# Recurrent attention and two feed-forward layers on one core: S of both batch halves in one step, a last group of sixteen, and a new order

## The chip, the core and the metric

The kernel runs on one core of a Trainium2 chip. Its engines are TensorE (PE in the profile; its weight loads are PEld), VectorE (DVE), ScalarE (ACT), GpSimd (POOL) and the DMA queues, which SyncE (SP) issues for the most part. The metric is the time of one execution on the device in microseconds; a number of runs is given by its median.

## The reference

```python
for t in range(S):                      # B, H, S, D = 2, 8, 768, 40
    m_new = np.maximum(f_gate[:, :, t] + m, i_gate[:, :, t])
    f_stab, i_stab = np.exp(f_gate[:, :, t] + m - m_new), np.exp(i_gate[:, :, t] - m_new)
    C = f_stab * C + i_stab * outer(v[t], k[t]);  n = f_stab * n + i_stab * k[t];  m = m_new
    y[:, :, t] = sigmoid(o_gate) * (C @ q[t]) / max(abs(n @ q[t]), 1)
x = y as (1536, 320)
x = ((x @ w1) * (x @ w2)) @ w3 @ w_out      # w1, w2: 320 x 1024; w3: 1024 x 1024; w_out: 1024 x 320
h = x @ w_in                                # 320 x 2048
out = (h * tanh(softplus(h))) @ w_out2      # 2048 x 320
```

All in float32. In lines 3 to 5 the indices are shortened.

## The kernel before

The sequence is cut into six chunks of 128 steps; a chunk of one of the two batch halves is a unit, so there are twelve (unit 2c + b is chunk c of half b). Per unit TensorE makes E (exponents of the decay, lines 618 to 625), S (products of k and q, lines 645 to 651: eight products on 40 rows, two heads at a time in the two halves of the array), I (state times q), U (the state's update, 40 columns, two at a time), Y (weights times v) and X (transposes). ScalarE takes the exponential of E into w (dw), VectorE multiplies S into w (wg, lines 653 to 656) and adds up the state, GpSimd makes vw, the gating by o and, from unit 8 on, the mask. Two units make 256 columns of a block of 512 tokens; there are three blocks.

The first layer then runs with float32 split into a rounded high and a low part: A and B (psa, psb, lines 1066 to 1076) are x with w1 and w2, W (psw) is w3 with w_out, X1 (psx) brings them together. The second layer (from line 1159) has 48 matrices of 128 by 512, sixteen in each block: H (psh, lines 1163 to 1187) makes two at once in the two halves of the array, ScalarE applies mish twice (line 1191 in the rounded format, line 1195 in full), VectorE takes the difference (gl), and O (pso, lines 1201 to 1213) multiplies both with w_out2 into four banks. They go in groups of eight: H of four pairs, then eight O (lines 1228 to 1241). Each weight piece is loaded and cleaned up on ScalarE and VectorE; its rounded half is made on ScalarE (hi), its low half on VectorE or GpSimd by a table (ENG).

The order on every engine is set by a planner when the program is built (Work.plan, lines 247 to 345). Each step is a node with an engine, a duration, what it depends on and which slots it takes; among the nodes that could start within a slack of each other, the one with the smallest due time goes first. Due times stand in the table DUE or come from formulas. The planner knows of three forms of products on TensorE (whole array, half rows for S and H, few columns for U) and adds SWITCH where the form changes. Where it sees TensorE waiting, up to the last X, it puts filler products into bank b0 (keep_warm, lines 589 to 594, psz in the profile), whose result nobody reads:

```python
stop = t + (s - t) * TUNE["ff"]
while t + 2 * fill[1] < stop:
    t, k = self.products(t, fill[1], 0.94), k + 1
while k < 12 and guard and self.lacks(t, max(s, t), max(s, t) + last, self.share[n]):
    t1, t, k = t, self.products(t, fill[1], 0.94), k + 1
```

The second loop adds fillers where the planner's own account of TensorE's load would go under the value gd; it is zero here.

Of the kernel before, what the change touches and what calls it, by code (L numbers as in the profile page):

```python
# [19 lines left out]
NQK = 2  # L20
# [6 lines left out]
    sgg=(2, 4), mu=8, s_pe=0.268, s_act=0.368, s_dve=0.435, s_pool=0.232, ahead=1, w0n=5, ff=0.972, gd=0.0,  # L27
    ph=0.071, a0=-12.81, ap=-93.853, a_ld=-1652.39, e_e=8363.2, e_s=3345.95, e_r=2252.59, g_ld=6316.58,
    g1=-2898.98, g2=-4276.68, o_1=-7529.36, o_2=8885.52, c_ld=3037.46, c_wo=1113.52, cp_wo=108.045, p0=-952.74,
    pp0=59.804, c_12=-11722.61, w0=1316.87, wp=-59.276, c_w3=-13157.38, p1=-662.73, pp1=33.908, p2=704.76,  # L30
    pp2=572.165, x0=-2337.92, x_p=2487.93, x1=-2214.51, x2=2869.52, xp=-139.242, ldn={'w12': 2, 'wi': 2},
    c_o2=88.35, cp_o2=12.531, c_wi=-5894.32, c_o3=-2264.6, m0=232.0, grp=8, mp0=-162.897, mp=204.465, m_o=1263.83,
# [4 lines left out]
    lo_w3='POOL', lo_wi='POOL', lo_o2='DVE', lo_o3='DVE', xo='POOL', vw='POOL', dup='ACT', rb0='DVE', rc0='DVE',  # L37
    rb1='DVE', rc1='DVE', rb='ACT', rc='ACT', st0='DVE', cb0='DVE', prep='ACT', g_tt='DVE', g_ll='DVE',
    lo_w120='DVE', lo_w121='DVE', lo_w122='DVE', lo_w123='DVE', lo_w124='DVE', lo_w125='POOL', lo_w126='DVE',
# [5 lines left out]
    set_0=0.0, ld_o_0=0.6, ld_g=1.3, ld_qk_0=1.7, ld_kv_0=1.8, load_0=1.9, ld_o_1=4.6, lr_0=4.8, less_0=4.8,  # L45
    ll_0=4.5, la1_0=5.1, la0_0=5.4, rb_0=5.4, one_0=5.7, lb0_0=38.2, lb1_0=6.2, pl_1=6.3, rc_0=6.4, pl_0=6.9,
    E_0=6.8, pa_1=7.7, pr_1=6.8, pa_2=7.8, E_1=8.1, dw_0=8.4, ld_qk_1=8.7, pt_1=9.0, S_0=9.0, pt_2=9.4,
    ld_kv_1=21.3, pb_1=10.6, dw_1=10.7, pb_2=10.8, pc_1=11.4, pc_2=11.7, te_1=11.9, lr_1=11.9, turn_1=12.3,
    less_1=13.1, te_2=13.2, lr_2=14.2, less_2=13.5, load_1=13.3, turn_2=13.9, ll_2=13.9, la1_2=14.1, ll_1=14.5,
    sgm_0=14.7, ld_o_2=14.7, vw_0=14.7, lb1_2=13.6, U_0=-9.8, ld_qk_2=16.0, rb_1=11.7, wg_0=16.7, la0_2=16.0,  # L50
    sgm_1=17.3, vw_1=17.4, ld_kv_2=17.1, la1_1=15.2, st_0=17.9, Y_0=18.0, la0_1=14.2, mag_0=17.3, lb0_2=18.4,
    lb0_1=19.0, set_1=19.1, lb1_1=-2.1, rc_1=19.4, S_1=19.9, clamp_0=20.0, rb_2=20.5, cb_0=20.6, load_2=20.6,
    E_2=20.9, wg_1=21.1, xs_0=31.7, r1_0=20.8, mag_1=21.3, E_3=22.0, ld_o_3=22.2, r2_0=17.9, bits1_0=11.3,
    dw_2=21.8, U_1=22.9, r3_0=24.9, bits2_0=25.1, Y_1=23.3, ld_qk_3=23.3, st_1=26.1, xo_0=23.9, bits_0=26.7,
    ld_kv_3=24.4, dw_3=24.0, S_2=25.2, cb_1=24.6, vw_2=25.5, r1_1=25.3, I_2=23.7, rc_2=25.6, wg_2=26.5, U_2=27.8,
    xs_1=27.4, dx_2=26.8, dup_0=25.2, Ie_2=30.6, hi_0=27.0, E_4=28.5, load_3=30.2, st_2=36.5, Y_2=29.4, dw_4=30.0,
    r2_1=27.8, lo_0=29.0, r3_1=29.8, mag_2=29.3, clamp_1=29.4, xo_1=30.5, X_0=31.2, ld_qk_4=30.7, cb_2=29.2,
    E_5=24.6, Xe_0=30.1, clamp_2=29.0, dup_1=32.7, r1_2=30.9, Xl_0=25.0, xs_2=31.7, S_3=32.4, dw_5=29.5,
    ld_kv_4=32.0, r2_2=28.1, bits1_2=32.5, ld_o_4=33.0, I_3=33.4, r3_2=33.0, vw_3=33.1, bits2_2=33.7, X_1=34.5,
    dx_3=33.4, U_3=34.9, rb_3=34.0, wg_3=34.6, xo_2=35.8, Xe_1=35.1, Ie_3=36.2, Y_3=36.7, st_3=36.2, rc_3=35.9,  # L60
    ld_qk_5=36.6, Xl_1=37.1, dup_2=37.0, bits_2=37.7, S_4=31.0, ld_kv_5=38.0, cb_3=38.5, vw_4=35.9, hi_2=38.4,
    load_4=57.2, E_6=40.7, bits1_1=39.4, r1_3=39.2, r2_3=39.9, wg_4=40.2, xs_3=38.4, I_4=39.9, dw_6=35.6,
    ld_o_5=40.7, I_5=41.6, r3_3=55.0, ld_qk_6=41.2, dx_4=40.1, Ie_4=40.2, xo_3=41.4, Y_4=42.5, ld_kv_6=42.1,
    Ie_5=41.2, rb_4=41.9, lo_2=43.3, dx_5=58.4, dup_3=39.6, S_5=41.4, rc_4=43.9, cb_4=44.4, E_7=46.0, r1_4=44.2,
    bits2_1=45.2, mag_3=45.1, X_3=47.0, X_2=47.5, r2_4=44.8, dw_7=45.9, vw_5=43.9, r3_4=46.6, U_4=47.9,
    clamp_3=47.0, Xe_3=46.9, U_5=41.3, wg_5=46.9, Xe_2=47.3, sgm_2=47.7, ld_qk_7=31.9, st_5=47.7, Y_5=50.2,
    vw_6=49.4, ld_kv_7=49.4, st_4=50.2, Xl_3=52.0, S_6=51.9, cb_5=51.1, Xl_2=51.4, E_8=21.4, r1_5=45.7, xs_4=52.1,
    sgm_3=51.8, sgm_4=51.8, sgm_5=51.8, wg_6=39.5, A_0=53.4, dw_8=53.9, xs_5=50.9, ld_kv_8=25.0, r2_5=47.1,
    bits1_3=53.5, r3_5=49.7, vw_7=53.2, B_0=55.3, bits2_3=61.7, Ae_0=54.7, bits_1=55.6, I_7=57.1, ld_kv_9=56.1,
# [284 lines left out]
def dve(n):  # L354
    return 0.07 + n / 960
# [18 lines left out]
def kernel(  # L374
# [78 lines left out]
    def bank(name):  # L453
        return slot(psum, name, [128, 512])
# [892 lines left out]
```

## Time and profile before

| | us |
|---|---|
| three runs | 430.96, 420.09, 430.78 |
| their median | 430.78 |
| the profiled execution | 418.26 |
| its span | 416.5 |
| busy in the span: TensorE, VectorE, ScalarE, GpSimd | 409.1, 290.9, 198.1, 76.5 |

The span goes from the first to the last instruction of the profiled execution. The attention fills about its first 108 us, the first layer goes to 242, the second to the end. Matmuls overlap in the pipeline, so the time from start to start says what one costs; the duration in a row is longer.

### The profile page before, as it was taken

Reading aid. Unit: us, or ns where it says so; the run is one execution under the profiler, and the core shown is the slowest. Engines: PE = TensorE matmul, PEld = TensorE weight load, DVE = VectorE, ACT = ScalarE, POOL = GpSimd, SP = SyncE. Lnnn points to the kernel's source line nnn. Section 1 sums busy time; section 2 is a strip of 40 time slices with the busy share of each in tenths; the row PEclk is TensorE's granted clock in tenths of the full one; section 3 lists DMA queues with packets and bytes.
Section 4 is the critical chain, followed back from the end, with each engine's and each line's share of the span. In section 5 each row is a group of like instructions: output and inputs, shape, how many; then the busy total and the mean of one; then the engine's idle time right before and its main releaser. Section 6 shows DMA issues by size and latency. Waiting matters only on the chain.

```text
span 416.5 us, 7139 instructions
## 1 busy us (share of the span) xinstructions
PE 409.1 (98%) x2814; PEld 359.7 (86%) x2814; DVE 290.9 (70%) x527; ACT 198.1 (48%) x381; POOL 76.5 (18%) x78
## 2 busy tenths in 40 slices
PE   8899999999999999999999999999999999999996
PEld 5688888898888899988888888989989999889995
DVE  7989989998899959887999988889231041330221
ACT  8786976544534444452743366157051161340430
POOL 3144343345002232422001132300000000000000
PEclk9999999999999999999999999999999999999999
DMA  8965844542224533435324253420100000100002
GB/s 240 326 192 161 239 164 135 159 151 65 64 89 143 169 108 101 151 115 155 98 71 119 65 126 80 174 64 2 65 0 2 0 2 2 63 2 0 2 2 64
DMA packets 30497, 40.88 MB, mean 98 GB/s; under 512 B 1856, under 2 KB 24640, under 8 KB 30464
## 3 DMA queue, kind: packets, MB, share of 16 engines
q1 hardware_dynamic: 29952, 39.95, 31.5%
q10 hardware_dynamic: 512, 0.48, 0.3%
q8 instruction: 22, 0.36, 0.3%
q14 instruction: 11, 0.09, 0.1%
HBM read 38.45 MB, written 1.97 MB: 97 GB/s over the span
## 4 chain that ended last, share of the span: by engine, by line
PE 93%; DVE 4%; ACT 1%; DMA 1%; issue 0%; DVEq 0%
PE pso L1210 21%; PE psh L1186 20%; PE psa L1057 11%; PE psb L1057 11%; PE psw L1028 7%; PE psY L699 5%; PE psS L650 3%; PE psx L1097 3%; PE psx L1099 3%; PE psx L1098 3%; PE psI L661 2%; PE psx L1102 1%; PE psx L1101 1%; PE psE L624 1%; PE psX L743 1%; PE psE L623 1%
## 5 line engine op out<-in xcount | busy, mean ns | idle before, releaser
L410 DVE TENSOR_TENSOR gl<-u,gh 128x512 fp32r<-128x512 f32 x48 | 32.8, 691 | 68.6 <-ACT u L1195 68.5
L1191 ACT ACTIVATE gh<-psh 128x512 fp32r<-128x512 f32 x48 | 28.9, 601 | 79.4 <-PE psh L1186 79.4
L1186 PE MATMUL psh<-xd,wih 64*128 64x512 f32 x240 | 59.7, 394 | 0.0
L1186 PEld LDWEIGHTS psh<-xd,wih 64*128 64x128 f32 x240 | 43.8, 185 | 3.4
L502 DVE SCALAR_TENSOR_TENSOR f<-raw,f 128x640 int32<-128x640 int32 (+2 forms) x44 | 42.4, 964 | 0.7
L1210 PE MATMUL pso<-wo,gh 128*128 128x320 f32 x192 | 42.6, 310 | 0.0
L1186 PE MATMUL psh<-hs,wih 64*128 64x512 f32 x144 | 41.7, 395 | 0.0
L507 DVE SCALAR_TENSOR_TENSOR f<-raw,f 128x640 int32<-128x640 int32 (+2 forms) x44 | 36.1, 823 | 0.9
L410 POOL TENSOR_TENSOR th<-f,th 128x512 fp32r<-128x512 f32 x16 | 21.4, 1345 | 64.9 <-ACT th L512 59.9
L1210 PEld LDWEIGHTS pso<-wo,gh 128*128 128x128 f32 x192 | 32.0, 188 | 1.1 <-issue 1.1
L1186 PE MATMUL psh<-xd,wil 64*128 64x512 f32 x120 | 31.8, 391 | 0.0
L1186 PE MATMUL psh<-hs,wil 64*128 64x512 f32 x120 | 31.6, 391 | 0.0
L1210 PE MATMUL pso<-wo2h,gh 128*128 128x320 f32 x96 | 30.0, 312 | 0.0
L1210 PE MATMUL pso<-wo2h,gl 128*128 128x320 f32 x96 | 29.6, 309 | 0.0
L1210 PE MATMUL pso<-wo2l,gh 128*128 128x320 f32 x96 | 29.6, 309 | 0.0
L1210 PE MATMUL pso<-wo,gl 128*128 128x320 f32 x96 | 29.6, 309 | 0.0
L1195 ACT ACTIVATE u<-psh 128x512 f32<-128x512 f32 x48 | 29.0, 604 | 0.0
L1186 PEld LDWEIGHTS psh<-hs,wih 64*128 64x128 f32 x144 | 26.1, 184 | 3.2 <-issue 1.3
L1057 PE MATMUL psa<-hs,w12h 128*128 128x512 f32 x72 | 28.5, 395 | 0.0
L1057 PE MATMUL psb<-hs,w12h 128*128 128x512 f32 x72 | 28.4, 394 | 0.0
L1028 PE MATMUL psw<-woh,th 128*128 128x320 f32 x128 | 28.3, 309 | 0.0
L493 DVE TENSOR_SCALAR f<-f 128x640 f32<-128x640 f32 (+2 forms) x44 | 22.7, 517 | 6.6 <-ACT f L487 5.8
(146 smaller groups left out, 1028.5 us busy)
## 6 DMA issues: line engine op xcount, KB each, us to landing
raw<-in_w_dram SPq DMA_DIRECT2D x16, 512.0 KB
raw<-in_w_out_dram SPq DMA_DIRECT2D x12, 640.0 KB
raw<-in_w_dram SPq DMA_DIRECT2D x16, 384.0 KB
raw<-in_w_in_dram SPq DMA_DIRECT2D x16, 320.0 KB
kv<-in_kv_dram SPq DMA_DIRECT2D x12, 324.0 KB
qk<-in_qk_dram SPq DMA_DIRECT2D x24, 160.0 KB
sg<-in_o_gate_dram SPq DMA_DIRECT2D x12, 160.0 KB
out_dram<-yo SPq DMA_DIRECT2D x9, 160.0 KB
```

The source lines that it names most:

```text
L410: return eng.tensor_tensor(out=o, in0=a, in1=b, op=op)
L493: nc.vector.tensor_scalar(out=ff, in0=ff, scalar1=HI_MIN, scalar2=HI_MAX, op0=ALU.max, op1=ALU.min)
L502: nc.vector.scalar_tensor_tensor(out=f, in0=t["raw"][:, :, 1], scalar=-0x40000000, in1=f, op0=ALU.bitwise_and, op1=ALU.bitwise_or)
L507: nc.vector.scalar_tensor_tensor(out=f, in0=t["raw"][:, :, 0], scalar=29, in1=f, op0=ALU.logical_shift_right, op1=ALU.bitwise_or)
L650: nc.tensor.matmul(t["S"][g][:, p * T:(p + 1) * T], lhsT=t["qk"][rows, 1, p, :], rhs=t["qk"][rows, 0, p, :], start=True, stop=True)
L699: nc.tensor.matmul(ps[:, h * VW:(h + 1) * VW], lhsT=t["w"][:, h, :], rhs=t["v"][:, h, :], start=True, stop=True)
L1028: nc.tensor.matmul(ps, lhsT=t[a][:, 0, c * 128:(c + 1) * 128], rhs=wo[b], start=(c0 + c + s == 0), stop=(c0 + c == KC - 1 and s == 2))
L1057: nc.tensor.matmul(ps, lhsT=a, rhs=b, start=(n == 0 and not begun), stop=(n == len(seq) - 1))
L1186: nc.tensor.matmul(mt[i + k]["ps"], lhsT=w[k][:, c], rhs=x[k][c], start=(n == 0 and c == 0), stop=(n == 2 and c == KC2 - 1))
L1191: nc.scalar.activation(out=t["gh"], in_=t["ps"], func=AF.Mish)
L1195: nc.scalar.activation(out=t["u"], in_=t["ps"], func=AF.Mish)
L1210: nc.tensor.matmul(ps, lhsT=t[a][:, sl], rhs=wo[b], start=(ft == 0 and n == 0), stop=(ft == KF2 - 1 and n == 2))
```

## The change

- S of both halves of a chunk is one step from chunk 2 on (ss=2): it waits for the loads and the E of both units and takes four banks.
- The groups of the second layer are 0-8, 8-16, 16-24, 24-32 and 32-48 instead of six of eight; the last one's matrices get the slots of the dead first-layer result as well.
- The planner counts 0.2 us for a change of form instead of 0.1, prefers to stay in a form (fb), fills all of a wait that it sees (ff) and guards its account of the load (gd=0.299).
- The low halves of the last four w_out2 pieces are made on GpSimd, those of two w1/w2 pieces change places.
- The table DUE has new values, above all for the attention.

```diff
 TUNE = dict(
-    sgg=(2, 4), mu=8, s_pe=0.268, s_act=0.368, s_dve=0.435, s_pool=0.232, ahead=1, w0n=5, ff=0.972, gd=0.0,
+    sgg=(2, 4), mu=8, s_pe=0.301, s_act=0.359, s_dve=0.435, s_pool=0.0, ahead=1, w0n=5, ff=1.0, gd=0.299, ph=0.071,
...
-    c_o2=88.35, cp_o2=12.531, c_wi=-5894.32, c_o3=-2264.6, m0=232.0, grp=8, mp0=-162.897, mp=204.465, m_o=1263.83,
+    x0=-2337.92, x_p=2487.93, x1=-2214.51, x2=2869.52, xp=-139.242, ldn={'w12': 2, 'wi': 2}, c_o2=88.35,
+    cp_o2=12.531, c_wi=-5894.32, c_o3=-2264.6, m0=232.0, grp=(0, 8, 16, 24, 32, 48), mp0=-162.897, mp=204.465,
+    m_o=1263.83, ss=2, sw=0.2, fb=3.0,
...
 ENG = dict(
-    lo_w3='POOL', lo_wi='POOL', lo_o2='DVE', lo_o3='DVE', xo='POOL', vw='POOL', dup='ACT', rb0='DVE', rc0='DVE',
+    lo_w3='POOL', lo_wi='POOL', lo_o2='DVE', lo_o3='POOL', xo='POOL', vw='POOL', dup='ACT', rb0='DVE', rc0='DVE',
...
 DUE = dict(
-    ld_kv_1=21.3, pb_1=10.6, dw_1=10.7, pb_2=10.8, pc_1=11.4, pc_2=11.7, te_1=11.9, lr_1=11.9, turn_1=12.3,
+    ld_kv_1=21.3, pb_1=10.6, dw_1=9.5, pb_2=10.8, pc_1=11.4, pc_2=11.7, te_1=11.9, lr_1=24.6, turn_1=12.3,
...
-                    c = min((c for c in cand if c[0] <= s0 + TUNE.get(SLACK.get(e), 0.0)), key=lambda c: c[1])
+                    stay = TUNE["fb"] if e == "PE" else 0.0
+                    c = min((c for c in cand if c[0] <= s0 + TUNE.get(SLACK.get(e), 0.0)),
+                            key=lambda c: c[1] - (stay if self.form[c[2]] == form else 0.0))
...
             if e == "PE" and self.form[n] != form:
-                last += self.SWITCH
+                last += TUNE["sw"]
...
         tag = work.take()
+        if tag[0] == "y":
+            k, n = divmod(int(tag[1:]), 5)
+            h, l = xset["b", k]
+            return (h[:, n] if n < 3 else l[:, n - 3]).bitcast(F32)
...
         def S_():
-            t["S"] = [bank("psS") for _ in range(2)]
...
+            for t in (tl[x] for x in mine):
+                t["S"] = [bank("psS") for _ in range(2)]
...
-        node("S", "PE", -K["e_s"], 0.9, S_, [("ld_qk", u), ("E", u), ("Y", u - K["ahead"])], [at("wg"), at("wg")],
-             warm=0.45, form=1)
+        mine = [x for x in range(u - u % B, u - u % B + B)] if c >= K["ss"] else [u]
+        if u == mine[0]:
+            node("S", "PE", -K["e_s"], 0.9 * len(mine), S_,
+                 [(x, n) for n in mine for x in ("ld_qk", "E")] + [("Y", u - K["ahead"])],
+                 [(AT, [("wg", n)]) for n in mine for _ in range(2)], warm=0.45, form=1)
...
-        node("wg", "DVE", -3, 2 * dve(512), wg, [("S", u), ("dw", u), ("vw", u), ("ms", u)])
+        node("wg", "DVE", -3, 2 * dve(512), wg, [("S", mine[0]), ("dw", u), ("vw", u), ("ms", u)])
...
+    def group(i):
+        return next((a, b) for a, b in zip(K["grp"], K["grp"][1:]) if a <= i < b)
...
-        p, g = i // 2, i // K["grp"]
+        p = i // 2
+        g0, g1 = group(i)
+        last = kb == NBLK - 1
+        GP = places("z", 16) + (places("z", 6, 25) + places("y", 10)) * last
+        YP = places("z", 16) if last else places("z", 6, 25)
...
-                     [("H", p - 1), ("X2l", kb), ("B", NBLK * KF1 - 1), ("lo", wi_n[ft // 2]), ("O", g * K["grp"] - 1)],
+                     [("H", p - 1), ("X2l", kb), ("B", NBLK * KF1 - 1), ("lo", wi_n[ft // 2]), ("O", g0 - 1)],
```

In the order of TensorE this is what the prediction speaks of. First, S of units 4 and 5 (rows of both qk buffers), with Y of unit 3 ahead. Before:

```order
L675 MATMUL psU<-vw,kv 40x41 x8
L594 MATMUL psz<-causal,identr 128x512 x5
L699 MATMUL psY<-kv,w 128x41 x8
L650 MATMUL psS<-qk_78 128x128 x8
L661 MATMUL psI<-st_80,qk_78 128x82 x4
L664 MATMUL psI<-ex_r_90,ones_92 128x8
...
L699 MATMUL psY<-kv,w 128x41 x8
L675 MATMUL psU<-vw,kv 40x41 x8
L650 MATMUL psS<-qk_79 128x128 x8
```

After:

```order
L682 MATMUL psU<-vw,kv 40x41 x8
L668 MATMUL psI<-st_80,qk_78 128x82 x4
L671 MATMUL psI<-ex_r_90,ones_92 128x8
L600 MATMUL psz<-causal,identr 128x512 x2
L706 MATMUL psY<-kv,w 128x41 x8
L657 MATMUL psS<-qk_78 128x128 x8
L657 MATMUL psS<-qk_79 128x128 x8
...
L750 MATMUL psX<-ident,x 128x128 x3
L706 MATMUL psY<-kv,w 128x41 x8
```

Both S stand together behind Y of unit 3, where I, E, I, Y and U stood between them; the fillers ahead of Y of unit 3 are two and not five, and stand behind an I. Second, the stretch from U of units 5 and 4 on, after the change (before, it holds no filler):

```order
L682 MATMUL psU<-vw,kv 40x41 x16
L600 MATMUL psz<-causal,identr 128x512 x4
L682 MATMUL psU<-vw,kv 40x41 x8
L706 MATMUL psY<-kv,w 128x41 x8
...
L657 MATMUL psS<-qk_78 128x128 x8
L657 MATMUL psS<-qk_79 128x128 x8
L600 MATMUL psz<-causal,identr 128x512 x5
L630 MATMUL psE<-ex_r_90,ex_l_88 128x512 x2
L600 MATMUL psz<-causal,identr 128x512
L706 MATMUL psY<-kv,w 128x41 x8
L750 MATMUL psX<-ident,x 128x128 x3
```

Three groups of fillers, ten products, are new here. Third, the border between matrices 39 and 40 in the second layer, before:

```order
L1210 MATMUL pso<-wo2h,gl 128x320
L1186 MATMUL psh<-hs_925,wih 128x512
L1186 MATMUL psh<-xd,wih 128x512 x2
...
L1186 MATMUL psh<-xd,wil 128x512
L1210 MATMUL pso<-wo_3023,gh 128x320 x2
L1210 MATMUL pso<-wo_3023,gl 128x320
```

These two borders, from O to H and back to O, are gone after the change: H of matrices 32 to 47 runs without an O in between, and so do their sixteen O.

## Rows read from the trace of the kernel before

**Rows 1.** The page, parts 1 and 2: busy us, share, instructions; granted clock by slice.
```profile
PE 409.1 (98%) x2814; PEld 359.7 (86%) x2814; DVE 290.9 (70%) x527; ACT 198.1 (48%) x381; POOL 76.5 (18%) x78
...
PEclk9999999999999999999999999999999999999999
```

**Rows 2.** The page, part 4: the chain of waits by engine.
```profile
PE 93%; DVE 4%; ACT 1%; DMA 1%; issue 0%; DVEq 0%
```

**Rows 3.** Busy us of PE, PEld, DVE, ACT, POOL by stretch; clock, DMA.
```profile
18.76:53.26 34.50, 34.04 (x353) 29.72 (x352) 32.13 (x73) 28.05 (x67) 13.44 (x15) 1.00 0.69 204
...
107.73:412.62 304.89, 304.85 (x1953) 271.76 (x1951) 192.74 (x322) 126.82 (x226) 34.85 (x24) 1.00 0.23 69
```

**Rows 4.** PE in order of time: start, us, line, operation.
```profile
42.15 0.47 PE L623 MATMUL psE<-causal,identr 128*128 128x512 f32 x1
42.46 0.40 PE L624 MATMUL psE<-ex_r,ex_l 128*128 128x512 f32 x1
...
44.08 1.96 PE L699 MATMUL psY<-kv,w 128*128 128x41 f32 x16
45.97 0.51 PE L675 MATMUL psU<-vw,kv 128*40 128x41 f32 x16
46.40 1.16 PE L650 MATMUL psS<-qk 40*128 40x128 f32 x16
47.49 0.51 PE L623 MATMUL psE<-causal,identr 128*128 128x512 f32 x1
47.84 0.39 PE L624 MATMUL psE<-ex_r,ex_l 128*128 128x512 f32 x1
48.07 0.39 PE L623 MATMUL psE<-causal,identr 128*128 128x512 f32 x1
...
53.26 0.50 PE L1057 MATMUL psa<-hs,w12h 128*128 128x512 f32 x1
...
57.02 1.01 PE L661 MATMUL psI<-st,qk 128*128 128x82 f32 x8
```

**Rows 5.** PE in order of time, at borders of H and O groups.
```profile
255.82 0.39 PE L1186 MATMUL psh<-xd,wil 64*128 64x512 f32 x1
256.14 0.42 PE L1210 MATMUL pso<-wo2h,gh 128*128 128x320 f32 x1
256.40 0.31 PE L1210 MATMUL pso<-wo2l,gh 128*128 128x320 f32 x1
256.54 0.31 PE L1210 MATMUL pso<-wo2h,gl 128*128 128x320 f32 x1
...
270.19 0.31 PE L1210 MATMUL pso<-wo2h,gl 128*128 128x320 f32 x1
270.43 0.50 PE L1186 MATMUL psh<-hs,wih 64*128 64x512 f32 x1
...
270.77 0.61 PE L1186 MATMUL psh<-hs,wih 64*128 64x512 f32 x2
271.00 0.62 PE L1186 MATMUL psh<-xd,wih 64*128 64x512 f32 x2
```

**Rows 6.** PE in order of time, Y of unit 3: idle before, releaser.
```profile
38.34 1.75 PE L699 MATMUL psY<-kv,w 128*128 128x41 f32 x14 [0.18 <-DVE w L410]
```

**Rows 7.** DVE in order of time: w of unit 3; a low half.
```profile
37.01 1.28 DVE L410 TENSOR_TENSOR w<-psS,w 128x512 f32<-128x512 f32 x2
...
289.85 0.82 DVE L410 TENSOR_TENSOR wo<-f,wo 128x640 fp32r<-128x640 f32 x1
```

**Rows 8.** POOL groups by form: count, busy us, mean ns, idle before.
```profile
L410 POOL TENSOR_TENSOR wil<-f,wih 128x640 fp32r<-128x640 f32 x8 | 13.4, 1686 | 64.2 <-ACT wih L512 64.2
```

**Rows 9.** Chain in order of time: start, us, what.
```profile
284.63 14.28 PE pso L1210 x96
```

**Rows 10.** PE in order of time: fillers early in the span.
```profile
4.37 3.35 PE L594 MATMUL psz<-causal,identr 128*128 128x512 f32 x7 [0.35 <-ACT causal L871]
...
16.78 2.14 PE L594 MATMUL psz<-causal,identr 128*128 128x512 f32 x8
```

More of the change, by code (lines that the diff above doesn't have):

```diff
@@ L50 @@
[L50 to L69, printed above, removed]
@@ new lines @@
+    r1_11=78.9, Xe_4=101.7, Xl_9=85.4, xs_11=113.0, Xl_4=101.5, xo_10=88.7, B_3=98.0, Be_2=94.7, dup_10=101.7,
+    r2_11=88.1, bits1_8=121.4, r3_11=99.9, bits2_8=128.3, B_4=69.1, Be_3=104.9, xo_11=98.1, bits_8=123.5,
+    dup_11=94.6, X_11=91.5, bits_7=153.2, load_10=80.9, X_10=102.8, Xe_11=90.3, B_5=99.3, Be_4=103.5, Xe_10=102.6,
+    hi_7=143.9, Xl_11=104.9, Xl_10=105.1, B_6=99.1, lo_7=131.2, late=104.1, Ph_0=109.6, Ph_1=104.7, Pl_0=106.3,
+    Ph_2=105.3, Pl_1=106.9, A_7=90.4, hi_8=128.6, Pl_2=106.1, load_11=99.2, mag_9=148.4, Be_5=107.2, Be_6=112.4,
@@ L178 @@
     UP, DOWN = 0.78, 0.3
-    SWITCH = 0.1
     PHASES = 4
@@ L645, in S_ @@
         def S_():
-            t["S"] = [bank("psS") for _ in range(2)]
-            for p in range(HP):
-                for g in range(2):
-                    rows = slice(64 * g, 64 * g + D)
-                    nc.tensor.matmul(t["S"][g][:, p * T:(p + 1) * T], lhsT=t["qk"][rows, 1, p, :],
-                                     rhs=t["qk"][rows, 0, p, :], start=True, stop=True)
+            for t in (tl[x] for x in mine):
+                t["S"] = [bank("psS") for _ in range(2)]
+                for p in range(HP):
+                    for g in range(2):
+                        rows = slice(64 * g, 64 * g + D)
+                        nc.tensor.matmul(t["S"][g][:, p * T:(p + 1) * T], lhsT=t["qk"][rows, 1, p, :],
+                                         rhs=t["qk"][rows, 0, p, :], start=True, stop=True)
         def wg():
@@ L757, in add_unit @@
         at = lambda nm: (AT, [(nm, u)])
-        node("ld_qk", "SP", -K["a_ld"], 0.1, ld_qk, [("S", u - NQK), ("I", u - NQK), ("ld_qk", u - 1)], bytes=330e3)
+        node("ld_qk", "SP", -K["a_ld"], 0.1, ld_qk, [("S", u - NQK if c - NQK // B < K["ss"] else u - NQK - (u - NQK) % B), ("I", u - NQK), ("ld_qk", u - 1)], bytes=330e3)
         node("ld_kv", "SP", -K["a_ld"], 0.05, ld_kv, [("ld_kv", u - 1)],
@@ L1154 @@
     MH = places("b", 4)
-    GP, UP, YP = places("z", 16), places("z", 4, 16), places("z", 6, 25)
+    UP = places("z", 4, 16)
+    def group(i):
+        return next((a, b) for a, b in zip(K["grp"], K["grp"][1:]) if a <= i < b)
     acc = {}
@@ L1270 @@
             wo2_n[2 * i], wo2_n[2 * i + 1] = (n, 0), (n, 1)
-        G = K["grp"]
-        dues = [K["m0"] + (i // G) * G * 3.49 + (i % G) * 1.72 for i in range(NT)]
+        dues = [K["m0"] + group(i)[0] * 3.49 + (i - group(i)[0]) * 1.72 for i in range(NT)]
         for i in range(KF1):
```

102 lines of the change are left out of this document (58 added, 44 removed).

## The prediction

> **What bounds the kernel now.** I read the page first, then the chain of waits, then TensorE's busy time by stretch, then single rows of TensorE where the change touches it. The page has TensorE busy for 409.1 of the 416.5 us of the span and the granted clock at full in every slice [rows 1]. The chain of waits says the same in another way: 93% of it is TensorE, 4% VectorE, 1% ScalarE [rows 2]; its share of VectorE is the start and the last copy. By stretch [rows 3] TensorE works 34.04 of 34.50 us in the first part of the attention and 304.85 of 304.89 us in the layers. So from 18.76 us on it stands still for little more than 0.5 us, and the end is the sum of what its queue holds. VectorE is next: 32.13 of 34.50 us in the first of these stretches, so there it can become late, and later it has room.
>
> The profiled execution took 418.26 us, that is its span of 416.5 and 1.7 around it. This is 12.5 us under the median of the runs shown (430.78) and 1.8 under the shortest (420.09). My sum goes against 418.26; what the 12.5 us are is argued under the rivals, because no row of this execution holds them.
>
> **The change, part by part.** Work on TensorE stays the same but for three things that can be counted in the order of its instructions: fillers (psz), changes of tile form (S and H use half of the rows, U few columns, all else the whole array), and starts of a 512-column product behind the small fp32 products.
>
> *Fillers.* There are 37 before and 47 after. Up to the first Y both have 32 (7, 6, 2, 4, 8 with the five zr before; 8, 6, 1, 4, 8 with the same five), so that part costs nothing; it stands beside the gate work on VectorE. Behind the first Y there is one group of 5 before, and groups of 3, 2, 4, 5 and 1 after: 10 more. A 512-column product takes 0.23 us from start to start at full clock (47.84 to 48.07 us [rows 4]). As TensorE has no idle time there to hide them in, 10 x 0.23 = **+2.3 us**. If they stand in waits that the new order would have had anyway, they cost nothing: that bound is 2.3 us lower.
>
> *Changes of form.* At the border from O to H the first H product starts 0.24 us behind the last O one, against a pace of 0.14 to 0.15, and the next pair 0.34 behind it, against 0.23: 0.09 + 0.11 = 0.20 us. From H to O it is 0.32 against 0.23 and 0.26 against 0.14: 0.21 [rows 5]. S shows the exit by itself: the E product behind it takes 0.35 from start to start, 0.23 is normal (47.49, 47.84, 48.07 us [rows 4]). So I take 0.20 for one change. In the order I count 12 runs of S, 8 of U and 6 of H before, with two places where S and U touch: 2 x 26 - 2 = 50 changes. After, there are 8 runs of S (four single, four double), 8 of U, 5 of H, and four places where S and U touch: 2 x 21 - 4 = 38. 12 x 0.20 = **-2.4 us**, of which the last group of sixteen brings 0.4 and S with U 2.0.
>
> *Starts of 512-column products.* E behind I takes 0.31 instead of 0.23 to the next start (42.15, 42.46 us [rows 4]), 0.08 more. Such places, where a 512-column product follows I, Y or X, go from 9 to 15: **+0.5 us**.
>
> *New waits.* The waits for data before the change are of 0.18 us, Y on the product of S and w from VectorE [rows 6]; behind a step S come two such VectorE products, 1.28 us together [rows 7]. After the change S of the second unit is queued behind four pairs of E, and each double S puts four VectorE products in one go, so Y of the first half has 1.3 us of cover (two pairs of E and X) for 1.28 us of VectorE work plus the hand-over. What is queued behind a waiting Y is all of TensorE. From below: nothing. From above: at each of four double steps VectorE is one pair of products later than planned, 4 x 1.28 = 5.1 us. I take four waits of the size that the trace has, **+0.8 us**, since the planner that sets the order puts fillers where it sees a longer one.
>
> *Low halves of the last w_out pieces on GpSimd.* Four of them move from VectorE (0.82 us each [rows 7]) to GpSimd, where the same shape takes 1.686 [rows 8]. The third is needed by the fifth O of the second group: the group's eight take 14.28 us from 284.63 [rows 9], so this O comes at 284.63 + 4 x 1.785 = 291.8. VectorE starts on the low half at 289.85 and ends at 290.7 [rows 7]; on GpSimd it would end at 291.5, in front of the need. Nothing, with 0.9 as the upper bound. SP gets the same loads, with some kv loads earlier and the last qk load behind a weight load; what they wait for is not the bound here.
>
> *The sixteen in one group.* H and O themselves are the same products. The H part becomes 28 us without an O, and its mish passes and differences go to slots that stay held until that O; ScalarE and VectorE have room for them (busy for 126.82 and 192.74 of 304.89 us in the layers [rows 3]). The tail behind the last O does not change.
>
> Sum: +2.3 - 2.4 + 0.5 + 0.8 = +1.2 us, between -1.9 (fillers free, no new waits: -2.4 + 0.5) and +6.4 (all waits, GpSimd late: 2.3 - 2.4 + 0.5 + 5.1 + 0.9). So with the clock at full, the changed kernel takes 418.26 + 1.2 = **419.5 us**.
>
> **What the clock does.** The first filler products, before TensorE has been busy for some time, run 7 in 3.35 us; eight of the same at 16.78 us take 2.14 [rows 10]. That is 0.48 against 0.27 us each: the lower level of 1.2 GHz, then 2.4. So a stretch at the lower level takes nearly twice its time, and in this kernel nothing hides it. Where could the median execution lose 12.5 us? Between 44.08 and the first full block of psa and psb (53.26 to 57.02) TensorE gets small products: Y and U with 41 columns, S with 128 [rows 4]. An execution in which the clock falls at 44.5 us and is back only behind that block at 57.0 loses 57.0 - 44.5 = 12.5 us, the size of the gap. That is an inference: the trace shows the clock at full here [rows 1]. It fits that 420.09, 430.78 and 430.96 lie in two heaps and not around one value. The change sets fillers into just this stretch: of the 15 behind the first Y, 12 lie between the I just ahead of Y of unit 3 and the first psa. So I forecast that the median execution keeps the clock: 419.5 us, against 430.78.
>
> The Trainium skill speaks against this: "TensorE: Matmul & The Clock Gate", section "HAM oscillation — how this bites in real kernels", lets the clock fall where the array is idle in gaps. By that rule no fall could come in a queue without idle time, the fillers would be 2.3 us for nothing, and whatever makes the 12.5 us would stay. Here the trace cannot decide, since it shows neither a gap nor a fall; the same page's Part 1 says that the monitor runs free of the kernel's start, which fits two heaps of times.
>
> **The rivals.**
> - *What lengthens the median execution stays* (the change does not do what it says): the fillers do not reach what makes the 12.5 us, or the new order is thin elsewhere. For it: ahead of Y of unit 3 the new order has X, I, X, S, U, I with only two fillers behind them, and no row shows that the clock is the cause. Against: the new order has three filler groups where the thinnest products were. 419.5 + 12.5 = 432.0; with a shorter fall, from 47.5 to 57.0, 429.0. No change by 2%.
> - *VectorE becomes the bound of the attention*: at 32.13 of 34.50 us [rows 3] it has 2.4 us of slack there. Price: the upper bound above, 418.26 + 6.4 = 424.7. No change by 2%. Against: no VectorE work is added.
> - *Slower*: the clock falls already in that X, I, X, S, U, I stretch, at about 36 us in the time of before, and comes back only behind the first psa block, 57.0 - 36.2 = 20.8 us later, all of it doubled: 419.5 + 20.8 = 440.3. This decides from a fall at 37.1 on or before, as 2% over the median is 439.4. Against: in the trace of before the stretch from 33 to 37 is no denser, and its clock stood.
>
> **How the numbers follow.** About 2% is what a measurement of this kernel can tell from no change: 422.2 to 439.4. The forecast (422.2 and less) has 0.55, the first rival 0.28, VectorE 0.12, the slower one 0.04; 0.01 is left. So faster 0.55, same 0.41, slower 0.04. The range goes from 416.4 (all fillers free, 418.26 - 1.9) to 429.0: it holds the forecast, VectorE and the third of the first rival with shorter falls, some 0.77. The forecast's own range is 416.4 to 422.2.
>
> **What the profile after would show.** Right: TensorE busy to within 1 us from 19 us on, the last O ending between 411.5 and 416; one border from O to H less, each at 0.20 us; double S in some 2.0 us where two single ones took 2.18 and more; clock at full throughout. Wrong: idle time of Y on w of over 0.5 us at a double S (VectorE); O waiting for GpSimd near 292 us; a stretch ahead of the first psa in which 512-column products take 0.43 to 0.48 us, which would be a fall; or run times that again lie in two heaps 12 us apart, which would put the cause outside the fillers.

## The result, and the profile after the change

| | before | after |
|---|---|---|
| runs taken with the result | 6 | 6 |
| median (range), us | 423.17 (418.56 to 430.96) | 423.8 (421.54 to 427.8) |
| profiled execution, span | 418.26, 416.5 | 427.8, 426.1 |
| its mean granted clock | 1.000 | 0.979 |

The changed kernel is slower by about 1%: ratio 1.0106, 95% interval 1.007 to 1.0141. (The ratios leave out runs that lie well above the fastest of their kernel; medians and ranges hold all runs.) The forecast was 419.5 us, and faster.

The page of the changed kernel, parts 1, 2 and 4, answers to [rows 1, 2]:

```profile
PE 416.7 (98%) x2824; PEld 366.3 (86%) x2824; DVE 293.5 (69%) x523; ACT 197.7 (46%) x381; POOL 87.5 (21%) x82
...
PEclk9899589999999999999999999999999999999999
...
PE 93%; DVE 5%; DMA 1%; issue 1%; ACT 0%; DVEq 0%
```

TensorE still sets the end, with 7.6 us more of busy time and ten instructions more. The clock line has two dips that the one of before does not have, in the second slice and in the fifth and sixth. The next view, busy time by stretch, answers to [rows 3]; its columns are the stretch, its length, the busy time and instructions of TensorE, weight loads, VectorE, ScalarE and GpSimd, the granted clock, DMA share and GB/s:

```profile
15.72:19.14 3.42, 3.42 (x23) 2.30 (x23) 3.16 (x6) 3.39 (x6) 1.01 (x1) 0.50 0.98 328
20.21:43.03 22.82, 22.75 (x235) 20.44 (x234) 21.62 (x45) 16.52 (x41) 9.19 (x10) 1.00 0.60 179
43.03:56.68 13.65, 13.65 (x85) 12.26 (x86) 7.59 (x16) 6.56 (x16) 3.05 (x4) 0.50 0.60 176
56.68:120.00 63.32, 63.14 (x498) 55.41 (x497) 55.89 (x112) 33.23 (x75) 27.01 (x26) 1.00 0.40 131
```

From 43.03 to 56.68 us the clock stands at 0.50, 1.2 GHz in place of 2.4, and TensorE has no idle time there: 13.65 of 13.65 us. Half of it, 6.8 us, is lost. A shorter fall, from 15.72 to 19.14 us, stands ahead of the first Y, which starts at 20.21 us and not at 18.76. The profiled execution is 6.3 us above the fastest of its kernel, so the two falls are all of that and somewhat more; of the fastest there is no profile to compare with. TensorE's instructions in order of time (start, us, operation), the place of [rows 4]:

```profile
39.11 0.71 PE L600 MATMUL psz<-causal,identr 128*128 128x512 f32 x2
39.66 1.87 PE L706 MATMUL psY<-kv,w 128*128 128x41 f32 x16
41.46 3.40 PE L657 MATMUL psS<-qk 40*128 40x128 f32 x32
44.79 0.79 PE L629 MATMUL psE<-causal,identr 128*128 128x512 f32 x1
45.38 0.63 PE L630 MATMUL psE<-ex_r,ex_l 128*128 128x512 f32 x1
45.81 0.63 PE L629 MATMUL psE<-causal,identr 128*128 128x512 f32 x1
...
55.52 1.72 PE L600 MATMUL psz<-causal,identr 128*128 128x512 f32 x4
```

Y of unit 3 with 41 columns and then S of units 4 and 5 with 128 columns follow each other for 5.1 us, and the clock falls in the second half of S. The E products behind it start 0.43 us apart, not 0.23. The two fillers stand ahead of this pair and not in it; the four at 55.52 run at the lower level themselves.

The second layer, from the chain in order of time (start, us, what), answers to [rows 9]:

```profile
280.08 14.14 PE psh L1201 x120
294.22 14.44 PE pso L1225 x96
...
365.49 28.08 PE psh L1201 x238
393.57 27.92 PE pso L1225 x189
```

The last group is there as forecast, one part H of 28.08 us and one part O. The O part at 294.22, whose late weight pieces now have their low half made on GpSimd, takes 14.44 against 14.28 us: the term that I set to nothing costs 0.16 us. The wait is for the last of the four pieces and not for the third (weight loads of TensorE in order of time):

```profile
305.01 0.19 PEld L1225 LDWEIGHTS pso<-wo,gh 128*128 128x128 f32 x1 [0.15 <-POOL wo L412]
```

At the start of the first layer one wait is new. TensorE, idle before and releaser in brackets:

```profile
162.73 0.50 PE L1109 MATMUL psx<-ph,w 128*128 128x512 f32 x1 [0.81 <-DVE w L412]
```

VectorE and GpSimd around it:

```profile
159.93 0.69 DVE L508 SCALAR_TENSOR_TENSOR f<-raw,f 128x512 int32<-128x512 int32 x1
160.65 1.69 DVE L513 SCALAR_TENSOR_TENSOR f<-raw,f 128x512 int32<-128x512 int32 x1
162.26 0.54 DVE L412 TENSOR_TENSOR w<-psw,w 128x256 fp32r<-128x256 f32 x2
```

```profile
160.50 1.29 POOL L412 TENSOR_TENSOR th<-f,th 128x512 fp32r<-128x512 f32 x1 [4.12 <-ACT th L518]
```

A cleaning step of a weight piece stands ahead of w in VectorE's queue, and beside GpSimd's product th (160.50 to 161.79) it takes 1.69 us, where the other 15 of its line and shape take 0.68 to 0.69. w starts when it ends, and X1 waits 0.81 us for w. The Trainium skill, "SBUF — State Buffer", section "SBUF: two separate sides", has VectorE and GpSimd share a pair of ports that one instruction holds to its end while the other is blocked; the trace agrees, since the step ends 0.55 us behind th, and a step of the same line that starts just ahead of a GpSimd product, at 197.23 us, takes 0.69 us.

### The profile page after: what moved, and what is told of

Same layout as the page of the kernel before. It is cut to its first block, busy times and chain, and to the rows that moved or that the text cites. A ratio compares the mean times of both kernels' runs of the same rounds, so it can differ in the third digit from the quotient of the medians.

```text
span 426.1 us, 7146 instructions
## 1 busy us (share of the span) xinstructions
PE 416.7 (98%) x2824; PEld 366.3 (86%) x2824; DVE 293.5 (69%) x523; ACT 197.7 (46%) x381; POOL 87.5 (21%) x82
## 4 chain that ended last, share of the span: by engine, by line
PE 93%; DVE 5%; DMA 1%; issue 1%; ACT 0%; DVEq 0%
PE pso L1225 20%; PE psh L1201 20%; PE psa L1067 10%; PE psb L1067 10%; PE psw L1038 6%; PE psY L706 5%; PE psx L1109 3%; PE psx L1107 3%; PE psS L657 3%; PE psx L1108 3%; PE psz L600 2%; PE psI L668 2%; PE psx L1112 1%; PE psx L1111 1%; PE psE L630 1%; PE psX L750 1%
## 5 line engine op out<-in xcount | busy, mean ns | idle before, releaser
L412 DVE TENSOR_TENSOR gl<-u,gh 128x512 fp32r<-128x512 f32 x42 | 28.7, 691 | 49.3 <-ACT u L1210 49.2
L1206 ACT ACTIVATE gh<-psh 128x512 fp32r<-128x512 f32 x42 | 25.2, 601 | 59.3 <-PE psh L1201 59.3
L508 DVE SCALAR_TENSOR_TENSOR f<-raw,f 128x640 int32<-128x640 int32 (+2 forms) x44 | 43.7, 992 | 0.8
L513 DVE SCALAR_TENSOR_TENSOR f<-raw,f 128x640 int32<-128x640 int32 (+2 forms) x44 | 36.4, 831 | 0.9
L412 POOL TENSOR_TENSOR th<-f,th 128x512 fp32r<-128x512 f32 x16 | 22.3, 1392 | 60.9 <-ACT th L518 60.2
L1235 DVE COPY yo<-pso 128x320 f32<-128x320 f32 x11 | 5.0, 491 | 37.4 <-PE pso L1225 37.4
L493 ACT ACTIVATE f<-raw 128x512 f32<-128x512 f32 (+2 forms) x28 | 21.1, 756 | 13.4 <-POOL th L412 6.8
L412 POOL TENSOR_TENSOR wil<-f,wih 128x640 fp32r<-128x640 f32 x8 | 13.4, 1683 | 64.2 <-ACT wih L518 64.2
L1201 PE MATMUL psh<-ls,wih 64*128 64x512 f32 x96 | 26.3, 389 | 0.0
```

What stands on the lines that cost most here:

```text
L412: return eng.tensor_tensor(out=o, in0=a, in1=b, op=op)
L493: nc.scalar.activation(out=t["f"].bitcast(F32), in_=t["raw"][:, :, 1].bitcast(F32), func=AF.Abs)
L508: nc.vector.scalar_tensor_tensor(out=f, in0=t["raw"][:, :, 1], scalar=-0x40000000, in1=f, op0=ALU.bitwise_and, op1=ALU.bitwise_or)
L513: nc.vector.scalar_tensor_tensor(out=f, in0=t["raw"][:, :, 0], scalar=29, in1=f, op0=ALU.logical_shift_right, op1=ALU.bitwise_or)
L1201: nc.tensor.matmul(mt[i + k]["ps"], lhsT=w[k][:, c], rhs=x[k][c], start=(n == 0 and c == 0), stop=(n == 2 and c == KC2 - 1))
L1206: nc.scalar.activation(out=t["gh"], in_=t["ps"], func=AF.Mish)
```

## The experiments

**The two kernels again**, unchanged, to see what their medians are.

> The kernel before, unchanged, to see its clock in every run. Theory (falls of TensorE's clock make the spread): runs with mean granted clock 1.000 take 418 to 419.5 us; the others are longer by about the span times (1 - clock), so 426 us goes with a clock near 0.98 and 431 with one near 0.97. Rival (something else makes the spread): long runs with a clock of 1.000.

> The changed kernel, unchanged, for a second profile and more runs. Theory: with the clock at 1.000 it takes 419.5 to 421.6 us, the excess over 419.5 being waits for VectorE that the profile with the fall hid; runs with falls are longer by about the span times (1 - clock), with the fall at the stretch from Y of unit 3 through the double S of units 4 and 5. Rival: the clock does not matter, and runs spread from 421.5 to 428 at 1.000.

Before: median 421.53 us (418.73 to 431.13, 12 runs), ratio 1.0009 [0.9976, 1.0043]. After: 423.28 (421.61 to 428.55, 11 runs), ratio 1.009 [1.006, 1.0121]. The kernel before was also run beside every other one. In these 74 runs its median is 419.8; 47 are under 421, 12 at 421.4 to 422.0, 6 at 424.7 to 426.4 and 9 at 430.8 to 431.4. These last have a mean granted clock of 0.968 where the shortest have 1.000. So the 430.78 that I took for the ordinary execution is met in one run of eight. The profile taken this time shows what such runs are made of (columns as in the view by stretch above):

```profile
18.98:41.08 22.10, 21.62 (x218) 18.76 (x219) 20.60 (x46) 16.88 (x41) 8.81 (x9) 1.00 0.70 203
41.08:58.15 17.07, 17.07 (x108) 15.17 (x104) 10.08 (x23) 8.64 (x22) 3.76 (x4) 0.50 0.48 149
```

It took 426.32 us. The clock is at 0.50 for 17.07 us, half of which (8.5) lies between this run and the fastest (418.3 + 8.5 = 426.8). The fall that the prediction inferred is real, starts 3.4 us earlier than I put it, and is shorter here. The Trainium skill, "TensorE: Matmul & The Clock Gate", section "HAM oscillation — how this bites in real kernels", ties such falls to gaps in which TensorE waits. Here the trace differs from the Trainium skill: in the low stretch and in the 2.4 us ahead of it TensorE was never idle, it worked through Y of unit 3 and S. The last wait ahead of that is the 0.18 us of Y on w, which the execution of [rows 6] has as well, without a fall. By that section of the Trainium skill, fillers in a queue without gaps could change nothing; the runs of before_fill below show that they do. What the falls in other runs have ahead of them is told with the reasons below.

**Fillers taken out of the changed kernel.** The 15 behind the first Y:

```diff
             if isinstance(n, int):
-                fill[0](n)
+                if s < 20:
+                    fill[0](n)
```

> The changed kernel without the 15 filler products behind the first Y, all else in the same order. Theory of the prediction (fillers cost 0.23 us each and hold the clock): runs at full clock 15 x 0.23 = 3.4 us shorter than the changed kernel's, about 417 to 418 us; but falls become longer or more frequent, so the slower runs reach 430 us. Rival 1 (they stand in waits): runs at full clock as long as with them, within 1 us. Rival 2 (they do nothing for the clock): the spread of the times and of the clock stays as it is, 3 us lower.

Median 434.21 us (423.21 to 446.87, 6 runs), 11 above the changed kernel. Two low stretches in the profile (433.4 us of span), 34.1 us in all:

```profile
27.12:40.77 13.65, 13.65 (x77) 12.45 (x77) 8.96 (x15) 5.26 (x14) 3.45 (x4) 0.50 0.45 133
...
57.84:78.32 20.48, 19.39 (x95) 17.89 (x95) 12.09 (x28) 11.78 (x29) 8.05 (x9) 0.50 0.38 118
```

So the fillers do hold the clock up at two places where the new order would lose it. What they cost at full clock this does not show: none of the six runs held the clock (the best, 423.21 us, has 0.992). Waits come into view where they stood (1.2 us on a load of qk, 0.8 on w, 0.6 on vw), 2.6 us against the 3.4 of 15 fillers, so some of their time is hidden in waits. The new order needs them; the old one had no such waits.

**The double S spread out again.** Each unit's S of units 4 to 7 by itself, the second one later; due times and fillers as in the changed kernel. The core of the edit, in the loop that issues the steps:

```diff
+            if late and (n == ("wg", late[0] + 1) or stands > 0):
+                late[1]([late[0] + 1])
...
+            if n in (("S", 4), ("S", 6)):
+                late[1]([n[1]])
+                continue
```

> The changed kernel with the second S of two double steps moved behind what follows it: E of unit 6 stands between S of units 4 and 5, and the five fillers between S of units 6 and 7; all else in the same order. Theory (the fall at 43 us comes from Y and two S in a row without a 512-column product): no fall near 43 us any more, so the slower runs go from 427 to 423 or less; at full clock 4 more changes of form, 0.8 us, so 420.5 to 422.5. Rival (the fall has to do with the early part or with chance): the spread stays 421.5 to 428, and the whole is 0.8 us longer.

Median 425.76 us (423.22 to 432.08, 6 runs), ratio 1.013 [1.0088, 1.0173]. There is no fall at 43 us in the profile, but one later:

```profile
54.98:75.46 20.48, 20.48 (x93) 18.01 (x94) 10.16 (x24) 9.55 (x25) 7.25 (x8) 0.50 0.33 104
```

The theory missed in its time: the slower runs did not go to 423 or less, two of six are at 432. Where the double S was taken apart the profiled execution has no fall, but a longer one came further on, right behind a wait of 0.7 us of I on a load of qk. One profile of each kernel cannot tell how often the fall comes in either place.

**One part of the change alone: the group of sixteen.** The kernel before with `grp=(0, 8, 16, 24, 32, 48)`, the function group and the slots that go with it; engines and due times as before.

> The kernel before with the last group of sixteen alone; attention, due times and the engines of the low halves as before. Forecast's term: two borders between O and H less at 0.20 us, so 0.4 us less at full clock: fastest run 417.9 to 418.1 against 418.3, and the stretch from the first H to the last O 169.9 to 170.1 us against 170.26. Rival (the long H part makes a slot or a pass late): an O of the last group waits, and the stretch is 170.3 or longer. In both cases the spread of the runs stays that of the kernel before, as the stretch before 60 us is the same: some runs 8 to 13 us above the fastest, with a granted clock of 0.97 to 0.98.

Median 418.71 us (418.28 to 426.42 in 11 runs; one at 460.56 with a granted clock of 0.83), ratio 0.9974 [0.9952, 0.9995]. From the chain in order of time:

```profile
355.84 28.08 PE psh L1193 x238
383.93 27.92 PE pso L1217 x189
```

From the start of the first H to that of the last O it is 169.85 us (242.11 to 411.96) against 170.26 (242.01 to 412.27): 0.41 less, the 0.4 of the forecast. In the fastest runs this does not show (418.28 against 418.26 of 74 runs), and the ratio's 0.26% is 1.1 us, more than the stretch gained: the rest is the spread of the runs.

**The other part alone: the double S with the old due times.** The kernel before with `ss=2` and the S step of the diff.

> The kernel before with S of both halves as one step from chunk 2 on, all due times as before. Theory 1 (the double S brings waits on w of VectorE that eat its saved changes of form, and thins TensorE's work): fastest run 419.5 to 421.5, above that of the kernel before by 1 to 3 us, idle time of 1 us or more on VectorE's products in the trace, and a median of 425 or more, since falls of the clock come in more of the runs. Theory 2 (the double S is good, and the new due times are what costs): four runs of S less and some meetings of S and U, 1.6 to 2.0 us less: fastest run 416.3 to 416.8, median at or under that of the kernel before.

Median 427.84 us (426.5 to 429.02, 6 runs), ratio 1.0184 [1.0152, 1.0217]. Theory 1 had the sign right, but not the size (its fastest run was to be 421.5 at most), and the waits were other ones. The view of waits (TensorE's line, releaser, us in total, times, longest):

```profile
PE psb L1061 <- ACT a L1076: 2.1, 1, 2.1
...
PE psY L700 <- DVE w L410: 1.3, 6, 0.4
PE psb L1061 <- DVE hs L410: 0.9, 1, 0.9
```

Y waits six times for w as the forecast feared, 1.3 us in all, of which the kernel before has 0.4; the larger waits, 3.0 us, are those of the first layer's products (psb), which are due earlier than their x and their bank are ready. The clock is at 0.50 from 96.38 to 103.20 us, which costs another 3.4. The new table of due times is not a tuning beside the double S: without it the double S is worse.

**The wait of X1 taken away from the changed kernel.** One cleaning step of VectorE is issued behind the first w:

```diff
+        turns = sorted(self.order)
+        names = [x[2] for x in turns]
+        a, b = names.index(("bits", 18)), names.index(("Wl", 0))
+        turns.insert(b, turns.pop(a))
-        for s, _, n in sorted(self.order):
+        for s, _, n in turns:
```

> The changed kernel, with one step of VectorE moved: the last cleaning step of the weight piece that stood ahead of the first w of the layers stands behind it now. Theory 1 (the 0.8 us of X1 on w are part of what the changed kernel lost at full clock): the idle time is gone, the fastest run is 420.4 to 420.9 and the ratio to the kernel before falls by 0.002 to 0.003. Rival (the wait moves on: the delayed piece is late for the next W): W waits for GpSimd's low half instead, and the fastest run stays at 421.3 to 421.8.

Fastest run 420.8 us against 421.54, median 424.99 (12 runs, to 435.57), ratio 1.009 [1.0054, 1.0126]. TensorE in order of time: X1 follows W with no wait now,

```profile
160.20 0.31 PE L1042 MATMUL psw<-wol,th 128*128 128x320 f32 x1
160.35 0.40 PE L1111 MATMUL psx<-ph,w 128*128 128x512 f32 x1
```

and from the first X1 to the second it is 8.90 us, as before the change, where the changed kernel has 9.97. So the wait of 0.81 cost 1.07. The two fastest runs (420.80, 420.84) are 0.7 to 0.8 under the two fastest of the changed kernel (421.54, 421.61). The ratio is that of after_again, so the 0.002 to 0.003 expected of it did not show, and the spread stayed, with two runs at 431.01 and 435.57. The profile has a fall that begins as a wait of I ends:

```profile
54.62 1.90 PE L672 MATMUL psI<-st,qk 128*128 128x82 f32 x8 [0.47 <-DVE f L517]
```

```profile
18.90:54.70 35.80, 35.13 (x361) 30.91 (x360) 33.90 (x71) 27.68 (x64) 11.71 (x13) 1.00 0.67 198
54.70:64.94 10.24, 10.24 (x55) 9.23 (x56) 6.18 (x14) 6.41 (x18) 3.39 (x4) 0.50 0.53 176
```

Through Y of unit 3 and the double S, at 39.43 to 43.68 us, the clock is at 1.00 here.

**More fillers in the order of before.**

```diff
             self.now = iter(self.place[n])
+            if n in (("S", 4), ("Y", 4), ("S", 5), ("Y", 5)):
+                fill[0](2)
             self.nodes[n][3]()
```

> The kernel before with eight more filler products, two each ahead of S of unit 4, Y of unit 4, S of unit 5 and Y of unit 5, in the stretch from 40 to 52 us in which its trace showed the clock fall. Theory 1 (the fillers hold the clock where it fell): 8 x 0.23 = 1.8 us more at full clock, fastest run 420.1 to 420.4, nearly all runs within 1.5 us of it, none above 425, and the profile at full clock from 20 us on. Rival (fillers do not reach the cause): the same 1.8 us, and still runs 8 to 13 us above the fastest, median 423 or more.

Eleven of 12 runs lie between 420.46 and 420.94 us, one at 423.84; median 420.72, ratio 1.0025 [1.0001, 1.005]. By stretch, where the run of before_again stood at 0.50:

```profile
41.50:55.81 14.31, 14.31 (x149) 12.32 (x145) 11.80 (x28) 11.47 (x26) 5.28 (x6) 1.00 0.67 198
```

The forecast's mechanism holds in the old order: fillers among the small products keep the clock, for 2.1 us (420.46 against 418.34, the fastest beside it; 0.26 each). But the median of the kernel before is only 1.5 us above its fastest run (419.8 against 418.3), so there was less to win than the fillers cost.

**Fewer fillers, with the group of sixteen.** As above, two ahead of S of unit 4, or two each ahead of S of units 4 and 5.

> The kernel before with the last group of sixteen and two filler products ahead of S of unit 4. Theory 1 (the fall behind that S is held off by little): 2 x 0.23 = 0.46 us more than with the sixteen alone, fastest run 418.4 to 418.8, and no run above 421. Rival (two are too few): the same fastest run, and some runs at 421 to 431 as in the kernel before.

> The kernel before with the last group of sixteen and four filler products, two ahead of S of unit 4 and two ahead of S of unit 5. Theory 1: 4 x 0.23 = 0.9 us and one more change of form at up to 0.2, so fastest run 418.9 to 419.4 and nearly all runs within 1 us of it; median 419.2, under the medians of both kernels (420.35 and 423.3). Rival (eight were needed): runs at 421 to 431 stay.

Two: median 419.44 us (418.8 to 422.34), ratio 0.9999 [0.9978, 1.002]. Four: 419.86 (419.51 to 423.02), ratio 1.0028 [1.0005, 1.005]; its fastest run is 0.1 above what was expected. In 12 runs each none was above 423.1, where the kernel before had 3 of 23 above 426 beside them. At the rate of the 74 runs (15 above 424) twelve runs would hold two or three such, so for two fillers alone this is likely and not certain; for two, four and eight together it is 36 runs with none. Runs at 422 to 424 stay now and then, where the theory had none above 421 for two.

**The changed kernel with enough fillers.** after_w_first with two each ahead of five steps:

```diff
+            if n in (("S", 4), ("Y", 4), ("Y", 5), ("I", 6), ("S", 6)):
+                fill[0](2)
```

> The changed kernel with w ahead of the cleaning step, as in the run before of that kind (fastest 420.8, median 425.0), and ten more fillers, two each ahead of the double S of units 4 and 5, Y of unit 4, Y of unit 5, I of unit 6 and the double S of units 6 and 7. Theory 1 (the spread of the changed kernel is falls of the clock in this stretch, and enough fillers end them): 420.8 + 10 x 0.23 = 423.1 or less where they stand in waits, nearly all runs within 1.5 us of the fastest, median under 425. Rival (the spread has to do with waits on VectorE): runs above 425 stay and the median is 426 or more, as the fillers come on top.

Median 422.74 us (422.36 to 424.38, 6 runs), ratio 1.0082 [1.0053, 1.0112]: the spread is down to 2 us in these six runs, and the median is 2.2 under that of the same kernel without them.

```profile
41.20:65.26 24.06, 24.06 (x242) 21.40 (x242) 21.13 (x44) 19.57 (x45) 10.07 (x11) 1.00 0.67 198
```

Clock 1.00 through the whole thin stretch. What is left against the kernel before is the cost of the order at full clock. The last O starts at 416.19 us, 3.9 later, and there are 20 fillers more behind the first Y. Added up from the start of each to the next start on TensorE, the 25 fillers take 6.93 us and the five of the kernel before 1.53: 5.4 more, 0.27 each. So all the rest is worth 1.5 us: the other products take 1.3 us less from the first Y to the first H, and 0.25 less from there to the last O.

**The price of a change of form.** In the kernel before, S of units 6 to 11 in two halves around the next step of TensorE:

```diff
+            if n[0] == "S" and n[1] >= 6:
+                self.nodes[n][3](range(2))
+                half = n
+                continue
...
+            if half and self.nodes[n][0] == "PE":
+                self.nodes[half][3](range(2, 4))
```

> The kernel before with S of units 6 to 11 cut in two halves of eight and eight instructions around the next step of TensorE: 12 more changes of form (62 instead of 50), no other work. Theory 1 (the forecast's price, taken from the borders of O and H, holds for S): 12 x 0.20 = 2.4 us, fastest run 420.5 to 420.9, and no idle time on w. Theory 2 (a change of form at S costs less than at the borders of O and H, so the changed kernel saved less than the 2.4 us of the forecast): 0.6 to 1.2 us, fastest run 418.9 to 419.5. Rival (w comes later, since S ends later): idle time of Y on w in the trace, to be taken off first.

Median 426.98 us (424.7 to 429.98, 6 runs), ratio 1.0182 [1.0137, 1.0227], far above both theories. The total is no measure of the price: the profile has the clock at 0.50 twice for 3.4 us, waits of X and of the first layer of 1.5 us in all, and other starts of psa. The price is read from single places at full clock. S of unit 9, E and psa, up to the next Y, before:

```profile
80.56 1.16 PE L650 MATMUL psS<-qk 40*128 40x128 f32 x16
81.66 0.73 PE L624 MATMUL psE<-ex_r,ex_l 128*128 128x512 f32 x2
82.22 0.39 PE L1057 MATMUL psa<-hs,w12h 128*128 128x512 f32 x1
...
84.07 0.31 PE L699 MATMUL psY<-kv,w 128*128 128x41 f32 x2
```

and in halves:

```profile
86.48 0.71 PE L660 MATMUL psS<-qk 40*128 40x128 f32 x8
87.12 0.73 PE L633 MATMUL psE<-ex_r,ex_l 128*128 128x512 f32 x2
87.78 0.72 PE L660 MATMUL psS<-qk 40*128 40x128 f32 x8
88.43 0.50 PE L1067 MATMUL psa<-hs,w12h 128*128 128x512 f32 x1
...
90.38 0.31 PE L709 MATMUL psY<-kv,w 128*128 128x41 f32 x2
```

3.51 and 3.90 us: 0.39 for two changes. The same sum for units 10 and 11 gives 0.32 and 0.40. So a change of form costs 0.16 to 0.20 us at S as well, and theory 1 holds for the price.

## Why the prediction was wrong

**The step that failed** is the one under "What the clock does": the 12.5 us between the profiled execution and the shown median were taken as something that the median execution loses, and the fillers as what gives it back. The first half fell with the count of runs. The median of the kernel before is 419.8 us over 74 runs, 1.5 above its fastest; the three runs shown held two of the rare long ones, by chance. With 419.8 as the base, even the forecast's own 419.5 would have been no gain that can be measured. That the measured 423.8 lies between 416.4 and 429.0 does not speak for the sum: that range was drawn to hold rivals as well, and the forecast's own part of it ends at 422.2.

**The second half was right as a mechanism and wrong for this order.** The clock does fall in that stretch (before_again), and fillers there hold it (before_fill). But the prediction went by where the 15 fillers stand, and not by what the new order puts between them: Y of unit 3 and a double S, 5.1 us of small products in one piece, with the fillers ahead of it. The fall starts in that piece in both profiles of the changed kernel (43.03 and 44.19 us). It needs no double S: in before_again it starts behind the same Y, in a single S. Of the 17 runs of after, five are 4 to 7 us above the fastest and none is 12; before has 9 of 74 up there, which would be two of 17, so that none came may be chance (after_w_first, with nearly the same order, has one at 435.57).

**What sets off a fall is open.** The profiles hold ten falls behind the first Y. Seven begin within 2.5 us of a wait of TensorE of 0.41 to 0.69 us, as the one of after_w_first above; in the other three (after, before_again, the first of before_halves) there is 0.18 us or less. So a fall does come in small products without such a wait. Whether short waits bring it about more often was not tried: after_held, which held the clock, has no wait over 0.2 us behind the first Y, so it does not tell the two apart. before_fill keeps the old order's wait of 0.18 us and holds the clock with fillers alone.

**The sum at full clock** was +1.2 and is +3.2 (421.54 at a granted clock of 1.000 against 418.34). Its counts hold: in the traces TensorE changes form 50 times before and 38 after, and has 9 and 15 such starts. By its terms:
- Fillers, +2.3: from the first Y to the first H the five of before take 1.53 us, from start to next start, and the 15 of after_again 4.00, so +2.5. How much of it the waits in after_no_fill would take back is not shown.
- Changes of form, -2.4, and starts of 512-column products, +0.5: a change is measured at 0.16 to 0.20, and 0.41 us for the last group against 0.4. In after_held, with 12 changes less and 10 starts more than before, the forecast's prices give -2.4 + 0.8 = -1.6, and all products but the fillers take 1.3 + 0.25 us less. The two terms hold together; no run tells the starts apart by themselves.
- New waits, +0.8: **mis-sized**. The forecast looked for them at Y behind the double S. X1 in the first layer cost 1.07 us, where nothing in the diff points to; it comes from the table's other times, by which a cleaning step and GpSimd's th meet ahead of w. Another is at the double S itself, which needs both of its loads and four banks. In after_again (TensorE, idle before in brackets):

```profile
43.31 1.24 PE L657 MATMUL psS<-qk 40*128 40x128 f32 x14 [0.61 <-DVE f L503]
```

  The releaser named is a cleaning step that S does not need. It is the load of the second qk: the last part of its second half landed at 43.18 us, by the semaphore that this product waits for, and TensorE's queue went on at 43.21. In the profile of after the load landed at 42.78 us and the same product started at 42.92, before the cleaning step ended at 43.34. From S to the E behind it is 3.16 us in after_again and 1.98 in after_held; 0.15 of the difference is the low clock from 44.19 us on, so the wait costs 1.0 us there. Other executions have less of it (2.45 us from S to E in after_w_first). The two make 2.1 us where the forecast had 0.8.
- Low halves on GpSimd, 0: 0.16 us, inside the bound of 0.9.

With these sizes the sum is +2.5 - 2.4 + 0.5 + 2.1 + 0.2 = +2.9, near the measured 3.2. The fastest runs have no profile, so whether they had the whole wait at S is not shown.

**The rivals.** "What lengthens the median execution stays" is what happened, with 429 to 432 us too high by the same wrong base. One of its two reasons held, that the new order is thin elsewhere, with only two fillers for Y of unit 3; the other, a doubt that the clock is the cause, did not. "VectorE becomes the bound" did not happen: it works 21.62 of 22.82 us in the first stretch, but the waits on it behind the first Y are X1's 0.81 us and, in after_again, 0.4 of an I and 0.2 of a Y. The fall in the X, I, X, S, U, I stretch of the slower rival did not come in the profiles of the changed kernel; without its fillers one began still earlier, at 27.12 us, and was over at 40.77, as that stretch began.

**The lowest median** is that of the kernel before with the last group of sixteen alone: 418.71, ratio 0.9974 [0.9952, 0.9995]. Its own gain is the 0.4 us of the second layer, and 3 of its 12 runs are above 426. With two fillers more it is as fast as the kernel before, but none of its 12 runs went above 422.4.

## What to carry to other kernels

Before a gap between a profiled execution and a median of a few runs is explained, count how often it comes: with two heaps of run times three runs say little of which one is the ordinary case. In this kernel fillers held TensorE's clock where they stood among the small products, and two ahead of a long piece of them did not, so read what the new order puts between them, and weigh their cost against the fall times its share of runs. A new order can cost a wait far from the edit: X1's wait on w, in the first layer, took 1.07 of the 3.2 us lost at full clock.

## What was not expected of the hardware

- The clock fell with TensorE busy without a gap, in 41-column and 128-column products (17.07 of 17.07 us busy at 0.50 in before_again, and none idle in the 2.4 us ahead of it). Most falls here do have a wait of 0.4 to 0.7 us close ahead of them.
- A wait costs more than its idle time: 1.07 us from X1 to X1 for 0.81 us of idle time shown, 0.26 more, and 1.0 us at the double S for 0.61.
- VectorE's cleaning step takes 1.69 us in place of 0.69 when it meets a GpSimd product of 1.29 that began before it, so that one GpSimd instruction off the path delayed TensorE.
